# A gated recurrence with a spectral mixing layer on one core: two more chunks in split float32r, gate sums on TensorE, constant matmuls, and another order

## Chip, core and metric

The kernel runs on one core of a Trainium2 chip. The metric is device time in microseconds of one execution; "before" is the median of three runs.

## What is computed

Four batches, eight heads, 768 positions, head size 48 (so 384 channels), all float32. A gated linear attention gives x, and x goes through a mixing layer:

```python
f = 1.0 / (1.0 + np.exp(-f_logit))
for t in range(S):
    state = f[:, :, t, :, None] * state + np.einsum('bhd,bhe->bhde', k[:, :, t], v[:, :, t])
    y[:, :, t] = np.einsum('bhd,bhde->bhe', q[:, :, t], state)
...
theta = x @ w_theta
zr, zi = x * np.cos(theta), x * np.sin(theta)
u = x + einsum('ts,bsd->btd', w_tok_r, zr) + einsum('ts,bsd->btd', w_tok_i, zi)
return u + np.maximum(u @ w_ch, 0.0)
```

The four weight matrices come as 8-byte floats and are turned into 4-byte floats by integer work on the chip.

## The kernel before

The 768 positions of each batch are six chunks of 128, so there are 24 chunks, numbered 0 to 23. Steps have two-letter names. For each chunk the program loads f, k, q and v ("lf", "lk", "lq", "lv"); clamps f from below ("gc", `gate_clamp`); takes log(1 + exp(-f)) ("go", `gate_open`, two ScalarE passes); sums it along the chunk by a VectorE scan ("gs", `gate_sum`); takes the falling and the rising exponential of the sum ("ge", `gate_exp`: `p` and, in place, `f`); multiplies q by the falling one ("gq") and k by the rising one ("gk"). "gp" keeps the last column of the falling product in `pes`. Then TensorE makes scores, key transposes and state sums ("sc", "ke", "up"), VectorE masks the scores and carries the state ("ma", "sa", "st", "sm"), TensorE makes the outputs ("qs", "ou") and turns x ("xt"), and x is kept as it is and turned ("xc", "xs").

The mixing layer's first product is "th" (`angles`), followed by rounding to a turn ("tn", "se", "ab"), sine and cosine ("tr") and the rotation ("ro"), which gives z. The products of z with the two token matrices ("f0", "f1", "f2" for three blocks of 128 channels; `products`) add up in PSUM for a group of 384 positions. VectorE adds them to `ut` ("v", line 462), the sum is split ("uh", "ul"), multiplied by the channel matrix ("c"), and finished and stored ("cv", "so").

A product is made in one of two ways. In plain float32 it is two TensorE instructions. In split form each operand has a high part in float32r and the remainder as a low part, and the product is three float32r matmuls: high by high, high by low, low by high. In the kernel before, `FULL = 1` keeps the whole first batch (chunks 0 to 5) in plain float32, and chunks 6 to 23 in split form. The split needs "xh", "xl" for x, "zh", "zl" for z, and "d4", "d5" for the weights. "d1", "d2", "d3" decode a weight part: shift the low words (VectorE), scale the high words (ScalarE), join (two VectorE instructions).

The order of all this is written out by hand: `ORDER` is a list of steps, and every engine's own queue, the loads on SP's queue among them, follows that list. A suffix /P, /D or /A puts a step on GpSimd (POOL), VectorE (DVE) or ScalarE (ACT). Tiles come from pools with few buffers: PSUM has four single banks (tag "b", used by "ke", "xt", "th", the product groups and "c"), `p` has one buffer, `f`, `k`, `q` and `v` three.

Of the kernel before, what the change touches and what calls it, by code (L numbers as in the profile page):

```python
# [92 lines left out]
def gla_moe_kernel(  # L93
# [111 lines left out]

    def split_hi(n):
        if parts[n][1] and not FULL:
            nc.scalar.mul(place(n, 1), values[n], parts[n][1])
        else:
            copy(nc.scalar, place(n, 1), values[n])  # L210

    def split_lo(n):
        if parts[n][1] and not FULL:
            nc.vector.scalar_tensor_tensor(place(n, 0), values[n], parts[n][1], place(n, 1),
                                           op0=ALU.mult, op1=ALU.subtract)
        else:
            on(nc.vector).tensor_tensor(place(n, 0), values[n], place(n, 1), op=ALU.subtract)
# [481 lines left out]
```

## Time and profile before

| | |
|---|---|
| median of three runs | 340.17 us (339.72 to 340.64) |
| the profiled execution, its own time | 340.03 us |
| its span, first to last instruction | 338.3 us |
| PE (matmul) busy | 320.4 us, 95% |
| DVE busy | 251.6 us, 74% |
| ACT busy | 188.7 us, 56% |
| POOL busy | 108.6 us, 32% |

The span is what the trace shows; the profiled execution's own time is 1.7 us more. A busy share is an average over the whole span. Matmuls overlap, and the trace models their ends, so that PE can read as busy while it waits up to a quarter of a microsecond; the distance from one start to the next tells its pace.

### The profile page before, as it was taken

The page shows a single profiled execution, that of the slowest core. Times are in us where ns is not written, and L with a number is a line of the kernel's source. Part 1 is how long each engine was busy: PE and PEld are TensorE (multiplying, and loading weights), DVE is VectorE, ACT ScalarE, POOL GpSimd, SP SyncE. Part 2 cuts the span into 40 slices and gives each one's busy share as a digit, 9 for nine tenths or more (in the row PEclk, how much of TensorE's full clock was granted, in tenths as well). Part 3 has the DMA queues.
Part 4 walks back from the last instruction along what each step waited for, and adds up shares of the span by engine and source line. Part 5 has one row for each costly group of instructions (what it writes and reads, how often), then busy time and mean ns, then how long its engine had stood idle before and what let it go on. Part 6 is the DMA issues. An engine that isn't in the chain of part 4 may idle for free. (4 is left out here: it accounts for less than half of the span.)

```text
span 338.3 us, 9998 instructions
## 1 busy us (share of the span) xinstructions
PE 320.4 (95%) x4320; PEld 283.2 (84%) x4320; DVE 251.6 (74%) x411; ACT 188.7 (56%) x308; POOL 108.6 (32%) x105
## 2 busy tenths in 40 slices
PE   0789999999999999999999999999999999999993
PEld 0676766776776789999999999999999999999992
DVE  5989999999999998898987857855437848534211
ACT  6787997995866755588476685244076114400010
POOL 3585152134418235701445423323212201300010
PEclk9999999999999999999999999999999999999998
DMA  7994994738761262374124320532121120000012
GB/s 256 382 401 168 317 372 151 249 114 323 244 224 30 64 230 82 91 233 141 33 85 149 122 79 2 187 114 84 40 73 48 47 73 27 0 2 0 11 60 78
DMA packets 21618, 45.54 MB, mean 135 GB/s; under 512 B 2368, under 2 KB 5440, under 8 KB 21568
## 3 DMA queue, kind: packets, MB, share of 16 engines
q1 hardware_dynamic: 21568, 44.84, 38.5%
q8 instruction: 36, 0.59, 0.7%
q14 instruction: 14, 0.11, 0.1%
HBM read 40.11 MB, written 4.72 MB: 133 GB/s over the span
## 5 line engine op out<-in xcount | busy, mean ns | idle before, releaser
L458 PE MATMUL pm<-wp,z 128*128 128x384 f32 x648 | 118.4, 337 | 0.0
L458 PEld LDWEIGHTS pm<-wp,z 128*128 128x128 f32 x648 | 112.4, 188 | 0.4
L458 PE MATMUL pm<-value,z 128*128 128x384 f32 x144 | 49.3, 487 | 0.0
L476 PE MATMUL pch<-uhl,wch 128*128 128x384 f32 x216 | 40.0, 337 | 0.0
L458 PEld LDWEIGHTS pm<-value,z 128*128 128x128 f32 x144 | 26.4, 190 | 15.2
L476 PEld LDWEIGHTS pch<-uhl,wch 128*128 128x128 f32 x216 | 37.4, 188 | 0.0
L469 POOL TENSOR_TENSOR uhl<-ut,uhl 128x384 fp32r<-128x384 f32 x13 | 14.2, 1094 | 67.0 <-ACT uhl L143 35.5
L236 POOL TENSOR_SCALAR f<-f 128x512 f32<-128x512 f32 x16 | 26.6, 1666 | 13.3 <-DMA f<-in_f_dram 12.5
L246 DVE TENSOR_TENSOR_SCAN f<-carry,f 128x512 f32<-128x512 f32 x24 | 29.8, 1246 | 1.4 <-ACT f L242 1.4
L257 POOL COPY pes<-p 128x4 f32<-128x4 f32 x24 | 10.5, 439 | 52.9 <-ACT p L253 52.9
L490 DVE SCALAR_TENSOR_TENSOR ut<-pch,ut 128x384 f32<-128x384 f32 x24 | 13.1, 550 | 18.8 <-PE pch L476 17.1
L308 PE MATMUL psk<-ident,k 128*128 128x128 f32 x96 | 16.9, 303 | 10.0 <-DVE k L266 10.0
L261 POOL TENSOR_TENSOR q<-q,p 128x512 f32<-128x512 f32 x12 | 17.3, 1446 | 23.1 <-ACT p L253 14.6
L462 DVE TENSOR_TENSOR ut<-pm,ut 128x384 f32<-128x384 f32 x24 | 13.0, 551 | 14.2 <-PE pm L458 14.2
L253 ACT ACTIVATE p<-f 128x512 f32<-128x512 f32 x24 | 15.1, 630 | 14.4 <-DVE f L246 6.8
L402 PE MATMUL pth<-wth,xh 128*128 128x384 f32 x108 | 23.0, 348 | 0.0
L308 PEld LDWEIGHTS psk<-ident,k 128*128 128x128 f32 x96 | 12.2, 153 | 12.3 <-issue 10.3
L435 DVE TENSOR_TENSOR w<-w,x 128x768 f32<-128x768 f32 x18 | 17.2, 962 | 6.3 <-ACT w L426 6.3
L143 ACT COPY x<-py 128x384 f32<-128x384 f32 x19 | 9.1, 478 | 22.5 <-PE py L361 22.1
L361 PEld LDWEIGHTS py<-v,sc 64*64 64x64 f32 x768 | 15.0, 140 | 7.4 <-issue 4.5
L143 ACT CAST uhl<-ut 128x384 fp32r<-128x384 f32 x7 | 3.6, 513 | 31.1 <-DVE ut L462 17.5
L266 DVE SCALAR_TENSOR_TENSOR k<-f,k 128x512 f32<-128x512 f32 x24 | 18.2, 758 | 1.8 <-ACT f L254 1.1
(83 smaller groups left out, 622.6 us busy)
## 6 DMA issues: line engine op xcount, KB each, us to landing
v<-in_v_dram SPq DMA_DIRECT2D x24, 384.0 KB, 4.3
f<-in_f_dram SPq DMA_DIRECT2D x24, 256.0 KB, 3.8
q<-in_q_dram SPq DMA_DIRECT2D x24, 256.0 KB, 4.1
k<-in_k_dram SPq DMA_DIRECT2D x24, 256.0 KB, 4.3
raw<-in_w_r_dram SPq DMA_DIRECT2D x12, 384.0 KB, 5.9
raw<-in_w_i_dram SPq DMA_DIRECT2D x12, 384.0 KB, 6.3
out_dram<-ut SPq DMA_DIRECT2D x21, 192.0 KB, 1.9
raw<-in_w_theta_dram SPq DMA_DIRECT2D x3, 384.0 KB, 6.4
```

The source lines that it names most:

```text
L236: on(nc.vector).tensor_scalar(ft, ft, F_MIN, None, op0=ALU.max)
L246: nc.vector.tensor_tensor_scan(fl, carry[:, pairs(h)].rearrange("p n t -> p (n t)"), fl, 0.0, ALU.mult, ALU.add)
L253: nc.scalar.activation(ps_[m][:, pairs(h)], ft, AF.Exp, scale=-1.0)
L261: on(nc.vector).tensor_tensor(qt, qt, ps_[m][:, pairs(h)], op=ALU.mult)
L266: nc.vector.scalar_tensor_tensor(kt, loaded["f", m][:, pairs(h)], E_TOP, kt, op0=ALU.min, op1=ALU.mult)
L308: nc.tensor.transpose(psks[m][:, p, :], loaded["k", m][:, p, :], ident)
L361: nc.tensor.matmul(out[HALF[t], j, p, :], scs[m][HALF[a], j, p, :], v2[HALF[a], t, p, :], start=(t == 0 and m % NC == 0 and p == 0), stop= ...
L402: nc.tensor.matmul(pths[m], l, r, start=(n == 0), stop=(n == len(ms) - 1))
L435: nc.vector.tensor_tensor(zs[m] if full else w, w, xs[m].unsqueeze(1).to_broadcast([P, 2, DM]), op=ALU.mult)
L458: nc.tensor.matmul(pms[g, d], l, r, start=(s == 0 and i == 0), stop=(s == NC - 1 and i == len(ms) - 1))
L469: on(nc.vector).tensor_tensor(us[g, d][:, 0], uts[g][:, d, :], us[g, d][:, 1], op=ALU.subtract)
L476: nc.tensor.matmul(pcs[g, d], l, r, start=(es[0] == 0 and n == 0), stop=(es[-1] == KD - 1 and n == len(ms) - 1))
```

## The change

- `FULL` now counts chunks and is 4: chunks 0 to 3 stay in plain float32, chunks 4 and 5 go the split way. Their weights for "th" and for the token products are split as well.
- `SUMMED = 4`: for chunks 0 to 3 f is loaded in a layout with the position on the partitions (a new input `ft`), and the sum along the chunk is a matmul with a triangle of ones (`upto`), four per chunk. The other chunks keep the scan.
- The clamp is gone. `gate_open` also writes row sums of exp(-f) to `opened`, and the check at the end looks at these too.
- The signs of the two exponentials change places: `p` now holds the rising product for k, `f` the falling one for q and for `pes`.
- `CUT = 1`: the gate work of chunk 0 is done in two halves of two head pairs each ("hlf", "hgo", "hgs" and so on).
- A new step "wu" (`keep_warm`) multiplies two constant tiles into a bank that nobody reads; it stands 30 times in the order.
- v is loaded as three parts of 192 columns, not twice 384: 288 KB a chunk, not 384.
- "d2" and "ro" may go to POOL.
- `ORDER` is new throughout.

```diff
-FULL = 1
-CUT = 0
+FULL = 4
+CUT = 1
+SUMMED = 4
...
     def gate_sum(m, h=None):
+        if m < SUMMED:
+            if not h:
+                sums[m] = bank([P, NP, C], f"psum{m}")
+            for p in range(NP)[pairs(h)]:
+                nc.tensor.matmul(sums[m][:, p, :], loaded["f", m][:, p, :], upto, start=True, stop=True)
+            return
         fl = loaded["f", m][:, pairs(h)].rearrange("p n t -> p (n t)")
...
-    def gate_clamp(m, h=None):
-        ft = loaded["f", m][:, pairs(h)]
-        on(nc.vector).tensor_scalar(ft, ft, F_MIN, None, op0=ALU.max)
...
-        nc.scalar.activation(ft, ft, AF.Exp, scale=-1.0)
+        n = B * NC if h else m
+        nc.scalar.activation(ft, ft, AF.Exp, scale=-1.0, accum_out=opened[:, n:n + 1])
         nc.scalar.activation(ft, ft, AF.Ln, bias=1.0)
...
-        nc.scalar.activation(ps_[m][:, pairs(h)], ft, AF.Exp, scale=-1.0)
-        nc.scalar.activation(ft, ft, AF.Exp)
+        nc.scalar.activation(ps_[m][:, pairs(h)], src, AF.Exp)
+        nc.scalar.activation(ft, src, AF.Exp, scale=-1.0)
...
+    def keep_warm(n):
+        nc.tensor.matmul(bank([P, C], f"warm{n}"), ident, carry[:, 1], start=True, stop=True)
...
-        vs[m] = sb.tile([P, 2, DM], F32, tag="v", bufs=3, name=f"v{m}")
+        vs[m] = sb.tile([P, 3, NP * D], F32, tag="v", bufs=3, name=f"v{m}")
...
-            products(g, s, d, zs[b * NC + s], b < FULL)
+            products(g, s, d, zs[b * NC + s], b * NC + s < FULL)
```

Of the new order three places are shown. The first is the head of PE's queue: `psk` is the transposed keys, `sk` the scores and state sums, `warm` a constant matmul, `psum` a gate sum. Before:

```order
L308 MATMUL psk_131<-ident,k_109 128x128 x4
L322 MATMUL sk<-v_111,ktok_136 64x48 x16
L297 MATMUL sk_156<-q_107,k_109 64x64 x16
L308 MATMUL psk_184<-ident,k_128 128x128 x4
L353 MATMUL py_216<-mid_191,q_107 64x48 x8
```

and now, from the tenth instruction on:

```order
L513 MATMUL warm_136<-carry,ident 128x128
L513 MATMUL warm_138<-carry,ident 128x128
L259 MATMUL psum_141<-upto,f_105 128x128 x4
L513 MATMUL warm_154<-carry,ident 128x128
L259 MATMUL psum_165<-upto,f_108 128x128 x4
L513 MATMUL warm_172<-carry,ident 128x128
L513 MATMUL warm_174<-carry,ident 128x128
L322 MATMUL psk_178<-ident,k_110 128x128 x4
L513 MATMUL warm_186<-carry,ident 128x128
L513 MATMUL warm_188<-carry,ident 128x128
L259 MATMUL psum_193<-upto,f_159 128x128 x4
L513 MATMUL warm_208<-carry,ident 128x128
```

The first key transposes, which opened the queue, now stand behind eleven constant matmuls in a row, two gate sums and three more constant ones.

The second place is the head of DVE's queue, behind its four small fills: `f` is the gate tile, `raw` the loaded words of a weight part (the first is of w_theta), `value` the decoded part. Before:

```order
L236 TENSOR_SCALAR f_92<-f_92 128x512
L236 TENSOR_SCALAR f_95<-f_95 128x512
L246 SCALAR_TENSOR_TENSOR f_92<-carry,f_92 128x512
L246 SCALAR_TENSOR_TENSOR f_95<-carry,f_95 128x512
L261 TENSOR_TENSOR q_107<-q_107,p_114 128x512
L266 SCALAR_TENSOR_TENSOR k_109<-f_92,k_109 128x512
L246 SCALAR_TENSOR_TENSOR f_104<-carry,f_104 128x512
L182 TENSOR_SCALAR raw_125<-raw_125 128x768
L266 SCALAR_TENSOR_TENSOR k_128<-f_95,k_128 128x512
```

and now:

```order
L191 TENSOR_SCALAR raw_96<-raw_96 128x768
L204 SCALAR_TENSOR_TENSOR raw_96<-raw_96 128x768
L205 SCALAR_TENSOR_TENSOR value_99<-raw_96 128x768
L191 TENSOR_SCALAR raw_117<-raw_117 128x384
L283 SCALAR_TENSOR_TENSOR k_110<-p_151,k_110 128x256
L283 SCALAR_TENSOR_TENSOR k_110<-p_151,k_110 128x256
L204 SCALAR_TENSOR_TENSOR raw_117<-raw_117 128x384
L205 SCALAR_TENSOR_TENSOR value_144<-raw_117 128x384
L278 TENSOR_TENSOR q_183<-q_183,f_105 128x256
L152 COPY ktok_199<-psk_178 128x512
L283 SCALAR_TENSOR_TENSOR k_161<-p_205,k_161 128x512
```

Clamps and scans are gone from the head, and the decoding of w_theta, whose load now stands first in SP's queue, has moved ahead of the first key product.

The third place is DVE's queue up to the first addition of a product group to `ut` (`pm` is such a group, `wth`, `wp` and `z` hold split parts). Before:

```order
L193 SCALAR_TENSOR_TENSOR value_986<-raw_901 128x768
L246 SCALAR_TENSOR_TENSOR f_990<-carry,f_990 128x512
L182 TENSOR_SCALAR raw_1165<-raw_1165 128x768
L143 CAST xh_1170<-ut_1122 128x384
L330 TENSOR_TENSOR mid_1176<-sk_1061,st_992 128x192
L334 TENSOR_TENSOR st_1182<-sk_1061,mid_1176 128x192
L246 SCALAR_TENSOR_TENSOR f_1007<-carry,f_1007 128x512
L182 TENSOR_SCALAR raw_1204<-raw_1204 128x768
L462 TENSOR_TENSOR ut_365<-pm_973,ut_365 128x384
```

and now:

```order
L456 TENSOR_TENSOR z_1239<-w_1059,z_1239 128x768
L204 SCALAR_TENSOR_TENSOR raw_1131<-raw_1131 128x768
L205 SCALAR_TENSOR_TENSOR value_1200<-raw_1131 128x768
L456 TENSOR_TENSOR z_1276<-w_1148,z_1276 128x768
L278 TENSOR_TENSOR q_956<-q_956,f_936 128x512
L278 TENSOR_TENSOR q_1084<-q_1084,f_1068 128x512
L343 TENSOR_TENSOR mid_1293<-sk_1112,st_1057 128x192
L347 TENSOR_TENSOR st_1295<-sk_1112,mid_1293 128x192
L191 TENSOR_SCALAR raw_1234<-raw_1234 128x768
L476 TENSOR_TENSOR ut_423<-pm_757,ut_423 128x384
```

The low parts of z for chunks 4 and 5 (line 456) now stand ahead of that addition, and two scans less do.

## Rows read from the trace of the kernel before

**Rows 1.** Busy time by stretch: us, then busy us of each engine, PEclk, DMA share, GB/s.
```profile
0.00:10.00 10.00, 0.45 (x2) 0.48 (x3) 5.90 (x11) 6.82 (x11) 3.06 (x12) 1.00 0.81 278
10.00:20.00 10.00, 8.92 (x207) 7.58 (x210) 9.23 (x16) 7.77 (x14) 7.55 (x7) 1.00 1.02 384
...
30.00:40.00 10.00, 10.00 (x217) 6.62 (x215) 9.38 (x15) 7.98 (x14) 4.67 (x4) 1.00 0.66 201
...
70.00:80.00 10.00, 10.00 (x161) 7.07 (x160) 9.90 (x14) 8.52 (x14) 1.89 (x2) 1.00 0.60 202
...
180.00:200.00 20.00, 20.00 (x336) 19.39 (x335) 14.88 (x23) 15.51 (x26) 9.30 (x8) 1.00 0.35 113
...
330.00:338.30 8.30, 2.64 (x16) 2.31 (x14) 1.64 (x3) 0.00 (x0) 0.19 (x1) 0.80 0.23 79
...
0.00:83.74 83.74, 71.66 (x1149) 49.66 (x1149) 76.17 (x119) 67.39 (x108) 34.07 (x41) 1.00 0.77 275
83.74:338.30 254.56, 248.75 (x3172) 233.54 (x3171) 175.48 (x294) 121.29 (x200) 74.50 (x65) 0.99 0.27 88
```

**Rows 2.** Timeline of PE: start us, us, instruction, count, idle time before it.
```profile
9.55 1.08 PE L308 MATMUL psk<-ident,k 128*128 128x128 f32 x4 [9.55 <-DVE k L266]
...
27.09 4.19 PE L402 MATMUL pth<-value,ut 128*128 128x384 f32 x6
...
34.54 2.20 PE L402 MATMUL pth<-value,ut 128*128 128x384 f32 x6
```

**Rows 3.** Costliest groups of the whole run: count, busy us, mean ns, idle before.
```profile
L458 PE MATMUL pm<-wp,z 128*128 128x384 f32 x648 | 118.4, 337 | 0.0
L458 PE MATMUL pm<-value,z 128*128 128x384 f32 x144 | 49.3, 487 | 0.0
L236 POOL TENSOR_SCALAR f<-f 128x512 f32<-128x512 f32 x16 | 26.6, 1666 | 13.3 <-DMA f<-in_f_dram 12.5
```

**Rows 4.** Groups of DVE from 0 to 83.74 us, the first L462 included.
```profile
L246 DVE TENSOR_TENSOR_SCAN f<-carry,f 128x512 f32<-128x512 f32 x12 | 15.2, 1279 | 1.0 <-ACT f L242 1.0
L193 DVE SCALAR_TENSOR_TENSOR value<-raw 128x768 int32<-128x768 int32 x9 | 8.9, 991 | 0.3
L192 DVE SCALAR_TENSOR_TENSOR raw<-raw 128x768 int32<-128x768 int32 x9 | 8.5, 948 | 0.0
...
L182 DVE TENSOR_SCALAR raw<-raw 128x768 int32<-128x768 int32 x11 | 6.9, 648 | 0.0
L435 DVE TENSOR_TENSOR z<-w,x 128x768 f32<-128x768 f32 x6 | 6.0, 1006 | 0.0
...
L236 DVE TENSOR_SCALAR f<-f 128x512 f32<-128x512 f32 x4 | 1.9, 463 | 2.3 <-DMA f<-in_f_dram 2.3
L409 DVE TENSOR_SCALAR w<-pth 128x384 f32<-128x384 f32 x3 | 1.6, 546 | 0.0
L143 DVE COPY ut<-pxt 128x384 f32<-128x384 f32 x3 | 1.6, 545 | 0.0
...
L143 DVE COPY ktok<-psk 128x512 f32<-128x512 f32 x1 | 0.7, 673 | 0.0
```

**Rows 5.** Groups of DVE of the whole run, for the split of z and of weights.
```profile
L442 DVE TENSOR_TENSOR z<-w,z 128x768 fp32r<-128x768 f32 x13 | 14.3, 1106 | 1.0 <-ACT z L143 0.9
...
L143 DVE CAST wp<-value 128x768 fp32r<-128x768 f32 x3 | 2.3, 776 | 0.0
```

**Rows 6.** Timeline of DVE: its first step on loaded data.
```profile
3.73 0.43 DVE L236 TENSOR_SCALAR f<-f 128x512 f32<-128x512 f32 x1 [2.14 <-DMA f<-in_f_dram]
```

**Rows 7.** DMA issues of the page: count, KB each, median us to landing.
```profile
raw<-in_w_theta_dram SPq DMA_DIRECT2D x3, 384.0 KB, 6.4
```

**Rows 8.** Waits of DVE from 3.7 to 83.7 us: total us, times, longest.
```profile
DVE f L246 <- ACT f L242: 1.0, 2, 0.7
DVE mid L330 <- PE sk L322: 1.0, 1, 1.0
...
DVE mid L328 <- PE sk L322: 0.6, 1, 0.6
DVE sc L303 <- PE sk L322: 0.5, 1, 0.5
```

More of the change, by code (lines that the diff above doesn't have):

```diff
@@ L98, in gla_moe_kernel @@
     f: bass.AP,
+    ft: bass.AP,
     v: bass.AP,
@@ L171, in hold @@
     def hold(n):
-        if FULL and n < NCH:
+        if n < NTOK or n < NCH and (n - NTOK) % NC < FULL:
             tag, bufs = ("uhl", 4) if n < NTOK else ("wp", 25)
@@ L186, in decode_high @@
         low, high = words(n)
-        nc.scalar.activation(high.bitcast(F32), high.bitcast(F32), AF.Copy, scale=2.0 ** -112)
+        if on(nc.scalar) is nc.scalar:
+            nc.scalar.activation(high.bitcast(F32), high.bitcast(F32), AF.Copy, scale=2.0 ** -112)
+        else:
+            on(nc.scalar).tensor_scalar(high.bitcast(F32), high.bitcast(F32), 2.0 ** -112, None, op0=ALU.mult)
     def decode_join(n):
@@ L204, in place @@
         return parts[n][2][i]
+    LATE = [n for n in range(NTOK, NCH) if (n - NTOK) % NC >= FULL]
+    SPLIT = [*range(NTOK), *LATE, *[n for n in range(NTOK, NCH) if n not in LATE]]
     def split_hi(n):
[L207 to L210, printed above, removed]
+        copy(nc.scalar, place(n, 1), values[n])
     def split_lo(n):
[L213 to L217, printed above, removed]
+        on(nc.vector).tensor_tensor(place(n, 0), values[n], place(n, 1), op=ALU.subtract)
     tables = []
@@ L249, in gate_exp @@
         ft = loaded["f", m][:, pairs(h)]
+        src = sums[m][:, pairs(h)] if m < SUMMED else ft
         gate_tables()
@@ L319, in att_state @@
             for j in range(2):
-                h = 2 * p + j
                 for t in range(1 if last_chunk(m) else 2):
                     nc.tensor.matmul(out[HALF[j], t, p, :], kts[m][HALF[t], p, HALF[j]],
-                                     vs[m][HALF[t], 0, h * D:(h + 1) * D], start=True, stop=True)
+                                     vs[m][HALF[t], j, p * D:(p + 1) * D], start=True, stop=True)
     def att_mid(m):
@@ L356, in att_out @@
     def att_out(m):
-        out, v2 = y_of(m), vs[m][:, 1, :].rearrange("s (t p e) -> s t p e", t=2, p=NP)
+        out = y_of(m)
         for n, (p, t) in enumerate(OUT):
@@ L360, in att_out @@
                 j = a ^ t
-                nc.tensor.matmul(out[HALF[t], j, p, :], scs[m][HALF[a], j, p, :], v2[HALF[a], t, p, :],
+                nc.tensor.matmul(out[HALF[t], j, p, :], scs[m][HALF[a], j, p, :],
+                                 vs[m][HALF[a], 2 * j, p * D:(p + 1) * D],
                                  start=(t == 0 and m % NC == 0 and p == 0), stop=(p == NP - 1))
@@ L434, in rotate @@
                 zs[m], zs[m + 1] = two[:, 0], two[:, 1]
-        nc.vector.tensor_tensor(zs[m] if full else w, w, xs[m].unsqueeze(1).to_broadcast([P, 2, DM]), op=ALU.mult)
+        on(nc.vector).tensor_tensor(zs[m] if full else w, w, xs[m].unsqueeze(1).to_broadcast([P, 2, DM]), op=ALU.mult)
     def split_zh(m):
@@ L494, in store @@
         nc.sync.dma_start(out[b, d * P:(d + 1) * P, th * TH:(th + 1) * TH], uts[g][:, d, :])
+    def keep_warm(n):
+        nc.tensor.matmul(bank([P, C], f"warm{n}"), ident, carry[:, 1], start=True, stop=True)
     flag = const.tile([P, 1], I32, tag="flag", name="flag")
-    worst = const.tile([P, 2], F32, tag="worst", name="worst")
+    worst = const.tile([P, 3], F32, tag="worst", name="worst")
     def find_worst(_):
         nc.vector.tensor_reduce(worst[:, 0:1], pes, axis=AX.XY, op=ALU.min)
-        nc.vector.tensor_scalar(worst[:, 1:2], worst[:, 0:1], E_MIN, None, op0=ALU.is_lt)
+        nc.vector.tensor_reduce(worst[:, 1:2], opened, axis=AX.X, op=ALU.max)
+        nc.vector.tensor_scalar(worst[:, 0:1], worst[:, 0:1], E_MIN, None, op0=ALU.is_lt)
+        nc.vector.scalar_tensor_tensor(worst[:, 2:3], worst[:, 1:2], G_TOP, worst[:, 0:1], op0=ALU.is_gt, op1=ALU.add)
         pf = bank([P, 1], "pf")
-        nc.tensor.matmul(pf[:1, :], ones, worst[:, 1:2], start=True, stop=True)
+        nc.tensor.matmul(pf[:1, :], ones, worst[:, 2:3], start=True, stop=True)
         nc.vector.tensor_copy(flag[:1, :], pf[:1, :])
@@ L514, in go @@
                 loaded[nm, m] = sb.tile([P, NP, C], F32, tag=nm, bufs=bufs, name=f"{nm}{m}")
-            nc.sync.dma_start(loaded[nm, m][:, pairs(h)], src[m // NC, m % NC][:, pairs(h)])
+            rows = ft[m] if nm == "f" and m < SUMMED else src[m // NC, m % NC]
+            nc.sync.dma_start(loaded[nm, m][:, pairs(h)], rows[:, pairs(h)])
         return go
     def load_v(m):
-        vs[m] = sb.tile([P, 2, DM], F32, tag="v", bufs=3, name=f"v{m}")
+        vs[m] = sb.tile([P, 3, NP * D], F32, tag="v", bufs=3, name=f"v{m}")
         nc.sync.dma_start(vs[m], v[m // NC, m % NC])
@@ L524, in inner, with later @@
         return lambda n: fn(n // (NC - 1) * NC + n % (NC - 1))
-    def later(fn, per, first=FULL):
-        return lambda n: fn(n + first * per)
+    def later(fn, first):
+        return lambda n: fn(n + first)
     def piece(d):
@@ L542, in gla_moe_kernel @@
     by_halves = {
-        "lf": load("f", f, 3), "lk": load("k", k, 3), "lq": load("q", q, 3), "gc": gate_clamp, "go": gate_open,
+        "lf": load("f", f, 3), "lk": load("k", k, 3), "lq": load("q", q, 3), "go": gate_open,
         "gs": gate_sum, "ge": gate_exp, "gq": gate_q, "gk": gate_k,
@@ L546, in gla_moe_kernel @@
     fn = {"h" + s: lambda n, go=go: go(n // 2, n % 2) for s, go in by_halves.items()}
-    fn |= {s: later(go, 1, CUT) for s, go in by_halves.items()}
+    fn |= {s: later(go, CUT) for s, go in by_halves.items()}
     fn |= {
         "lv": load_v, "lw": load_part,
-        "d1": decode_low, "d2": decode_high, "d3": decode_join, "d4": split_hi,
-        "di": decode_scale, "d5": split_lo,
+        "d1": decode_low, "d2": decode_high, "d3": decode_join, "d4": lambda n: split_hi(SPLIT[n]),
+        "di": decode_scale, "d5": lambda n: split_lo(SPLIT[n]),
         "e4": lambda n: split_hi(NCH + n), "e5": lambda n: split_lo(NCH + n),
@@ L555, in gla_moe_kernel @@
         "st": inner(att_new), "sm": inner(att_fade), "qs": att_old, "ou": att_out, "xc": att_x, "xt": att_turn, "xs": keep_x,
-        "xh": later(lambda m: split_xh(m, u_slice(m)), NC), "xl": later(lambda m: split_xl(m, u_slice(m)), NC),
-        "th": lambda m: angles(m, m < FULL * NC), "tn": whole, "se": settle, "ab": fold, "tr": trig,
-        "ro": lambda m: rotate(m, m < FULL * NC), "zh": later(split_zh, NC), "zl": later(split_zl, NC),
+        "xh": later(lambda m: split_xh(m, u_slice(m)), FULL), "xl": later(lambda m: split_xl(m, u_slice(m)), FULL),
+        "th": lambda m: angles(m, m < FULL), "tn": whole, "se": settle, "ab": fold, "tr": trig,
+        "ro": lambda m: rotate(m, m < FULL), "zh": later(split_zh, FULL), "zl": later(split_zl, FULL),
         "f0": piece(0), "f1": piece(1), "f2": piece(2), "v": group(add_u), "uh": group(split_uh), "ul": group(split_ul), "c": channels, "cv": group(finish),
-        "so": group(lambda g, d: store(g // NTH, g, d)), "fl": find_worst,
+        "so": group(lambda g, d: store(g // NTH, g, d)), "fl": find_worst, "wu": keep_warm,
     }
@@ L659, in rows @@
         return np.ascontiguousarray(t.transpose(0, 3, 2, 1, 4))
+    f = rows(inputs["f_logit"])
     v = np.asarray(inputs["v"])
@@ L664, in layout @@
     halves = v.transpose(0, 2, 1, 3).reshape(B, NC, 2, HF, NP, 2, D)
-    rolled = np.stack([np.stack([halves[:, :, t, :, :, a ^ t] for t in range(2)], axis=3) for a in range(2)], axis=2)
-    v2 = np.stack([halves.reshape(B, NC, C, DM), rolled.reshape(B, NC, C, DM)], axis=3)
-    v2 = np.ascontiguousarray(v2)
+    parts = [halves[..., 0, :], halves[..., 1, :], halves[:, :, ::-1, :, :, 1, :]]
+    v2 = np.ascontiguousarray(np.stack([a.reshape(B, NC, C, NP * D) for a in parts], axis=3))
     return {
@@ L670, in layout @@
         "k": rows(inputs["k"]),
-        "f": rows(inputs["f_logit"]),
+        "f": f,
+        "ft": np.ascontiguousarray(f.reshape(B * NC, P, NP, C)[:SUMMED].transpose(0, 3, 2, 1)),
         "v": v2,
```

17 lines of the change are left out of this document (11 added, 6 removed), and 72 rows, old and new, of the table ORDER.

## The prediction

> **What bounds the kernel now.** I read the stretches first, then PE's timeline, the groups, and DVE's waits. Read the stretches [rows 1] by column. PE does next to nothing in the first 10 us, is busy without a break from 30 us on, and ends in the last stretch. So from about 31 us to the end every microsecond of PE work is a microsecond of time. DVE is the second full engine: 9.23, 9.38 and 9.90 us of 10 in three of the stretches up to 80 us, but only 14.88 of 20 at 180 us. Two regimes follow. Up to about 84 us DVE and PE are packed together, and work taken off one of them alone need not help; later only PE counts. I cut the run at one place that both kernels have, the first addition of a product group to `ut`. Before it, DVE is busy 76.17 of 83.74 us; behind it 254.56 us are left, of which PE is busy 248.75 [rows 1].
>
> The head hides a third thing. Four key transposes from 9.55 us take 1.08 us, and the six angle matmuls at 27.09 us take 4.19 us, while the same six at 34.54 us take 2.20 [rows 2]. [...] The clock rose right behind a full-width stretch, the angle matmuls.
>
> **Products on PE.** A matmul of 384 columns occupies PE for 49.3/144 = 0.342 us in plain float32 and 118.4/648 = 0.183 us in float32r [rows 3]. One "f" step (a chunk, a block of channels) is four of the first kind, 1.37 us, or six of the second, 1.10 us. Two chunks, two groups and three blocks make 12 steps, so the split saves 12 x 0.27 = 3.2 us in all. A gate sum or a constant matmul moves 128 columns in two instructions: a third of 0.342 each, 0.23 us a matmul at the higher clock, 0.46 at the lower. The 16 gate sums add 3.7 us and the 30 constant ones 6.9 us. All the sums and 24 of the constants stand ahead of the place, most in the head, where PE is idle or waits: I cost them at nothing. If that cover is gone they cost up to 9.2 us (40 x 0.23).
>
> **DVE up to the place.** I count the instructions ahead of the addition in both orders and price them from [rows 4] and [rows 5]. Gone: six scans of twelve, 6 x 1.279 = 7.7; four clamps, 1.9; two roundings from `pth`, 1.1; one copy to `ut`, 0.5; one rotation, 1.0. Sum 12.2. Come in: one more join of a weight part, counted as three first halves more and one second half less, 3 x 0.948 - 0.991 = 1.9; a cast of a token part, 0.8, and one half its size, 0.4; one copy to `ktok`, 0.7; two low parts of z, 2 x 1.106 = 2.2. Sum 6.0. A few short ones of both signs (a fold less, half a q product more, a longer low part for a shorter one) cancel. Net: **-6.2 us**, or -5.7 when I allow 0.5 us for what the halved k products cost twice.
>
> **DVE's start.** Its first step on data was the clamp at 3.73 us [rows 6]. Now it is the shift of w_theta's words, behind two loads of 384 KB in place of one of 256. The extra 512 KB take 1.3 us at 384 GB/s, the rate from 10 to 20 us [rows 1]. Low end: 0.5 us, if the second load lands right behind the first. High end: w_theta took 6.4 us from issue to landing under load [rows 7], which from an issue at about 1.3 us is 4 us later than before. I take **+1.2**, near the low end, since only gate loads share the queue at that time.
>
> **DVE's waits up to the place.** The scans' wait for ACT, 1.0 us, goes with them. The waits for PE's `sk`, 1.0, 0.6 and 0.5 [rows 8], fall in the head, where PE ran at half its pace; with the higher clock I let them go, -2.1. New is a wait of the first join for POOL, which now scales the high words: no row shows that on POOL. Its clamp of 512 columns takes 1.666 us [rows 3], so 768 would be 2.5 us, against 0.65 us of shifting on DVE meanwhile [rows 4]: +1.9. Low end zero, high end 4, if the second part's scaling holds up a join as well. Together -1.0 - 2.1 + 1.9 = **-1.2**; between -3 and +3.
>
> **PE behind the place.** The new order leaves three "f" steps more behind it: two plain ones (2.74 us) and one split (1.10), +3.8. Seven split steps that already stood behind it save 7 x 0.27 = 1.9. Two constant matmuls in the middle add 0.5; the last four run behind the last channel products, beside DVE's last adds and the store, and cost nothing. Sum **+2.4**.
>
> **Other edits.** ACT is busy 67.39 of 83.74 us up to the place [rows 1]; row sums of the exponential and the extra high parts have 16 us of idle time to lie in. POOL is at 34.07 of 83.74, and its eight clamps there (8 x 1.666 = 13 us) make room for three scalings, two low parts and a rotation. The smaller loads of v and the larger check at the end touch no full engine. Without POOL's cover, a late state fade would come back as a DVE wait, which the range holds.
>
> **Sum.** -5.7 + 1.2 - 1.2 + 2.4 = -3.3. The profiled execution took 340.03 us (span 338.3, and 1.7 around it; its median of runs is 0.14 higher), so I predict **336.7 us**.
>
> **Rivals.** *First: DVE is no longer the bound.* DVE's 5.7 us, its 2.1 us of waits on a slow PE and all 3.2 us of products count, less 1.2 for the start and 0.5 for constants: -9.3, 330.7. For it: at 27 us PE spends 4.19 us on what takes 2.20, and gate sums let it start early. Against it: DVE at 9.90 of 10 us around 75 us [rows 1] cannot be run past. Half of it, 331 to 335, is likelier than all.
>
> *Second: nothing is left.* The new order puts more DVE work ahead of the twelfth chunk's key product than the old: four shifts, three joins, four token casts and two low parts of z more (2.6 + 5.8 + 3.1 + 2.2), four scans and four clamps fewer (-5.1 - 1.9), and some eight short ones of 0.4 to 1 us, about +10 us in all by [rows 4] and [rows 5]. PE has about as much less left behind it: five "f" steps (5 to 6 us), an angle product and one chunk's scores and state sums have moved ahead. If PE waits there, DVE's +10 and PE's -10 cancel and the later start of 1.2 us remains: 341.2, or 340 with the waits gone. For it: both engines are full up to the place [rows 1], so DVE's count decides. Against: not every DVE step ahead of those keys has to come before them.
>
> [...]
>
> [...]
>
> **How the numbers follow.** A measurement of this kernel tells 0.3%, about 1.0 us, from no change. Forecast (336 to 339): 0.45. First rival (331 to 336): 0.24. Second (339 to 341.2): 0.19. Third (above 341.2): 0.12. Faster by over 0.3% are the first two, less a little: 0.68; within 0.3% the second and the forecast's edge: 0.19; slower 0.13. The range 332.0 to 341.2 leaves out the third rival and the far end of the first.
>
> **What would show it.** Right: DVE's first addition to `ut` near 80 us (83.74 - 5.7 + 1.2 - 1.2 = 78), PE busy about 257 us behind it, angle matmuls of chunk 0 in 2.2 us instead of 4.19, and split products with `z` of chunks 4 and 5 at 0.18 us each. Wrong: PE waiting for DVE (`k`, `z`) between 80 and 130 us, as in the second rival; gate sums at 0.23 us an instruction, as in the third; a join that waits for POOL by more than 2 us; or the low words of w_theta landing after 6 us.

## The result, and the profile after

The changed kernel takes **343.38 us** (median of 4 runs, 342.0 to 344.7) against 339.95 of the kernel before on the same chip: ratio 1.0111, interval 1.0073 to 1.0148. It is slower by 3.4 us where 3.3 us less was forecast. Its profiled execution took 344.36 us, span 342.2. Ratios, here and below, compare the fast runs alone, each set with its own runs of the kernel before, so a ratio need not be the quotient of two medians.

The stretches, columns as in [rows 1]; the first three rows end at the first addition to `ut`, the place of the prediction:

```profile
0.00:30.00 30.00, 24.77 (x471) 21.25 (x472) 20.92 (x38) 21.76 (x46) 18.19 (x26) 1.00 0.86 308
30.00:70.00 40.00, 35.58 (x639) 24.95 (x640) 33.80 (x54) 33.28 (x58) 12.59 (x13) 0.96 0.72 232
70.00:84.82 14.82, 14.82 (x214) 11.72 (x210) 14.68 (x23) 11.92 (x20) 3.10 (x3) 1.00 0.65 217
...
0.00:84.82 84.82, 75.18 (x1307) 57.92 (x1311) 69.40 (x113) 66.96 (x122) 33.88 (x41) 0.98 0.76 256
84.82:342.20 257.38, 251.01 (x3147) 238.84 (x3139) 170.90 (x282) 120.70 (x207) 92.91 (x79) 0.99 0.26 83
```

The same cuts in the kernel before:

```profile
0.00:30.00 30.00, 18.01 (x328) 14.32 (x329) 24.12 (x39) 23.13 (x38) 15.43 (x23) 1.00 0.90 334
30.00:70.00 40.00, 39.92 (x653) 26.38 (x652) 38.45 (x62) 33.67 (x54) 13.75 (x14) 1.00 0.69 238
```

DVE is busy 69.40 us up to the place, 6.8 less than before [rows 1]: the work did go. But DVE is idle for 15.42 us there (84.82 - 69.40) against 7.57, and the place comes 1.1 us later, not 5.7 earlier. Of the 7.85 us of new idle time, 3.2 lie in the first 30 us (9.08 against 5.88) and 4.65 between 30 and 70 us (6.20 against 1.55). PE too, without a pause from 30 to 70 us before, now stands for 4.4 us there. The waits of DVE up to the place (total, times, longest), which answer to [rows 8]:

```profile
DVE raw L191 <- DMA raw<-in_w_theta_dram: 3.2, 1, 3.2
DVE k L283 <- ACT p L270: 2.7, 2, 2.0
DVE raw L204 <- POOL raw L199: 2.1, 1, 2.1
DVE mid L343 <- PE sk L335: 1.3, 1, 1.3
DVE sc L317 <- PE sk L335: 1.2, 1, 1.2
```

The timeline of PE tells why PE stands:

```profile
36.21 0.40 PE L335 MATMUL sk<-v,ktok 64*64 64x48 f32 x12
37.95 0.55 PE L335 MATMUL sk<-v,ktok 64*64 64x48 f32 x20 [1.34 <-issue]
38.43 2.20 PE L416 MATMUL pth<-value,ut 128*128 128x384 f32 x6
...
43.49 0.69 PE L311 MATMUL sk<-q,k 48*64 48x64 f32 x30
46.66 0.27 PE L311 MATMUL sk<-q,k 48*64 48x64 f32 x2 [2.48 <-issue]
...
47.88 3.46 PE L416 MATMUL pth<-value,ut 128*128 128x384 f32 x6
```

Read the two bracketed rows. Each stop lies inside a run of 32 equal products whose operands are all there: 30 of the scores' products run, nothing happens for 2.48 us, then the last two. "issue" is time in which the engine waited for nothing that the profile shows. Behind the second stop the granted clock falls to 0.50 (from 49 to 51 us; 0.92 from 40 to 50 as a whole, 0.91 from 50 to 60), and the angle matmuls need 3.46 us for what takes 2.20 at 38.43. The two DVE waits for `sk` end behind the two stops (38.55 and 47.50 us). The long wait for `p` comes later by a chain: PE's late outputs hold up ACT's copy `x`, ACT's queue stands behind it, and DVE's k product behind that. ACT:

```profile
53.68 0.48 ACT L152 COPY x<-py 128x384 f32<-128x384 f32 x1 [4.20 <-PE py L374]
54.17 1.28 ACT L234 ACT_TABLE_LOAD   x1
55.47 0.63 ACT L270 ACTIVATE p<-f 128x512 f32<-128x512 f32 x1
```

and DVE:

```profile
56.13 0.69 DVE L283 SCALAR_TENSOR_TENSOR k<-p,k 128x512 f32<-128x512 f32 x1 [2.03 <-ACT p L270]
```

The kernel before had a stop of the same kind, in a row that the prediction passed over:

```profile
21.70 1.10 PE L322 MATMUL sk<-v,ktok 64*64 64x48 f32 x31 [1.05 <-issue]
```

Part of the rest came about as announced. In this execution the head is quick on PE, with a granted clock of 1.00 on record from 7.5 us: chunk 0's angle matmuls take 2.20 us, against 4.19 [rows 2].

```profile
22.34 2.20 PE L416 MATMUL pth<-value,ut 128*128 128x384 f32 x6
```

The split products stand in their groups, at 0.187 us each where 0.183 was priced, and the plain ones at 0.356 against 0.342:

```profile
L472 PE MATMUL pm<-wp,z 128*128 128x384 f32 x720 | 134.7, 339 | 0.0
L472 PE MATMUL pm<-value,z 128*128 128x384 f32 x96 | 34.2, 493 | 0.0
```

So the two groups together are busy 168.9 us, against 167.7 [rows 3]: these rows do not show the 3.2 us saved. A group's busy time also holds the modelled ends of its matmuls. Counted instead from each product's start to the start of the next matmul, over all of the trace, the products take 158.45 us against 160.88, so 2.4 us were saved. The kernel now ends with PE's constants instead of DVE's last add (the chain that ended last):

```profile
335.88 0.47 PE warm L513 x2
```

### The profile page after: what moved, and what is told of

It is laid out like the page before. It is cut to its first block, busy times and chain, and to the rows that moved or that the text cites. A ratio compares the mean times of both kernels' runs of the same rounds, so it can differ in the third digit from the quotient of the medians.

```text
span 342.2 us, 10309 instructions
## 1 busy us (share of the span) xinstructions
PE 326.2 (95%) x4442; PEld 296.8 (87%) x4442; DVE 240.3 (70%) x393; ACT 187.7 (55%) x329; POOL 126.8 (37%) x119
## 5 line engine op out<-in xcount | busy, mean ns | idle before, releaser
L472 PE MATMUL pm<-wp,z 128*128 128x384 f32 x720 | 134.7, 339 | 0.0
L476 DVE TENSOR_TENSOR ut<-pm,ut 128x384 f32<-128x384 f32 x24 | 13.2, 552 | 31.1 <-PE pm L472 31.1
L472 PE MATMUL pm<-value,z 128*128 128x384 f32 x96 | 34.2, 493 | 0.0
L407 POOL TENSOR_TENSOR xl<-ut,xh 128x384 fp32r<-128x384 f32 x14 | 18.7, 1334 | 37.4 <-DVE xh L152 21.3
L456 POOL TENSOR_TENSOR z<-w,z 128x768 fp32r<-128x768 f32 x10 | 20.6, 2058 | 15.1 <-DVE z L152 13.6
L283 DVE SCALAR_TENSOR_TENSOR k<-p,k 128x512 f32<-128x512 f32 (+1 forms) x25 | 18.8, 754 | 8.2 <-ACT p L270 4.5
L416 PEld LDWEIGHTS pth<-wth,xh 128*128 128x128 f32 x120 | 21.0, 188 | 0.9 <-ACT ktok L152 0.2
L278 POOL TENSOR_TENSOR q<-q,f 128x512 f32<-128x512 f32 (+1 forms) x14 | 20.2, 1442 | 3.3 <-ACT f L271 2.5
L311 PE MATMUL sk<-q,k 48*64 48x64 f32 x768 | 16.9, 221 | 3.5 <-issue 2.5
L374 PEld LDWEIGHTS py<-v,sc 64*64 64x64 f32 x768 | 14.2, 133 | 6.2 <-issue 3.4
L249 ACT ACTIVATE f<-f 128x512 f32<-128x512 f32 (+1 forms) x25 | 15.3, 611 | 5.8 <-DMA f<-in_ft_dram 3.7
L311 PEld LDWEIGHTS sk<-q,k 48*64 48x64 f32 x768 | 14.1, 135 | 5.0 <-issue 4.2
```

Source lines behind the costliest of these rows:

```text
L249: nc.scalar.activation(ft, ft, AF.Exp, scale=-1.0, accum_out=opened[:, n:n + 1])
L278: on(nc.vector).tensor_tensor(qt, qt, loaded["f", m][:, pairs(h)], op=ALU.mult)
L283: nc.vector.scalar_tensor_tensor(kt, ps_[m][:, pairs(h)], E_TOP, kt, op0=ALU.min, op1=ALU.mult)
L311: nc.tensor.matmul(out[HALF[j ^ t], j, p, :], kt[r, p, HALF[t]], qt[r, p, HALF[t]], start=True, stop=True)
L374: nc.tensor.matmul(out[HALF[t], j, p, :], scs[m][HALF[a], j, p, :], vs[m][HALF[a], 2 * j, p * D:(p + 1) * D], start=(t == 0 and m % NC == ...
L407: on(nc.vector).tensor_tensor(xls[m], src, xhs[m], op=ALU.subtract)
```

## The experiments

Theory B: PE stops at fixed counts of its own instructions, and the order now puts such a stop into runs of small products. Theory A: the head starves DVE. Rivals: a collision with loads, and the constants' own PE time or clock. Steps are named as in the order (`wu` a constant matmul, `lw` a load of weights, `d1`, `d2`, `d3` the shift, scaling and join of their words, `lf`, `lk` loads, `go`, `gs`, `ge` the gate steps, `/P` on POOL, `h` half a chunk). All kernels but one are the changed one with the edit shown; the kernel before had a median of 339.5 to 340.1 us in each set.

**What the constants cost.** Three kernels take some of them out.

```diff
e2_tail
-c rv cv wu wu cv cv so wu wu
+c rv cv cv cv so
e4_nowarm
-wu   (all 30)
e8_eleven
-wu   (all but the first 11)
```

> The changed kernel without the last four constant matmuls. Theory 'fetch': they keep PE from its end by 1.4 us, so that its last instruction transfer comes behind the 576 KB store; without them the time from the last finishing add to the end falls from 6.9 us to the 5.6 us of before, 1.0 to 1.4 us faster. Theory 'idle': they run beside DVE's last adds and the store and cost nothing, within 0.3 us.

Measured 341.8 us (ratio 1.006, 1.003 to 1.009), 1.6 less than the changed kernel. The two intervals overlap, but the traces agree with the medians. DVE's last additions, in the changed kernel, in e2_tail and in the kernel before:

```profile
334.15 1.67 DVE L504 SCALAR_TENSOR_TENSOR ut<-pch,ut 128x384 f32<-128x384 f32 x3 [3.08 <-PE pch L490]
335.42 1.67 DVE L504 SCALAR_TENSOR_TENSOR ut<-pch,ut 128x384 f32<-128x384 f32 x3 [3.08 <-PE pch L490]
331.63 1.67 DVE L490 SCALAR_TENSOR_TENSOR ut<-pch,ut 128x384 f32<-128x384 f32 x3 [3.08 <-PE pch L476]
```

From their end to the end of the span it is 6.4 us (342.2 - 335.8) with the four constants, 4.8 without them (341.9 - 337.1), and 5.0 before. The last four constants were costed at nothing and cost that.

> The changed kernel without any constant matmul. [...] Theory 'DVE': the head waits for DVE anyway, and the whole is up to 1.5 us faster, by the tail and by the constants' own time. Rival 'gate sums warm enough': the clock rises with the gate sums, and the head differs by under 1 us.

Measured 339.45 us (0.9998, 0.9967 to 1.0028): 3.9 less than the changed kernel, where no theory gave more than 1.5. No wait on "issue" is left on PE, and DVE is busy 39.65 us of the 40 between 30 and 70.

> The changed kernel with only the first 11 of its 30 constants, those that run before 10 us. Theory B (constants cost where PE is full or where they move PE's instruction count; in an idle head they only lift the clock): 338.5 to 339.8, the angles of chunk 0 in 2.2 us, no wait of PE of 2 us amid the scores products near 44 us, since that run of products now ends before PE's 1473rd instruction. Rival (the 11 cost their share, by a chip that falls back in clock behind them or by later first steps): 340.5 to 342, with granted clock under 0.95 in a stretch before 60 us.

Measured 338.85 us (0.9946, 0.9917 to 0.9976): faster than the kernel before, 4.5 us less than the changed kernel. Behind the head one stop is left, and in PE's timeline it lies elsewhere, amid an angle product:

```profile
46.41 0.66 PE L322 MATMUL psk<-ident,k 128*128 128x128 f32 x4
46.91 0.81 PE L416 MATMUL pth<-value,ut 128*128 128x384 f32 x2
48.48 1.45 PE L416 MATMUL pth<-value,ut 128*128 128x384 f32 x4 [0.76 <-issue]
```

So far the constants could be at fault themselves. The next kernels part the loads, the constants and the count.

**Loads or count.** e1_spread moves four of the eight loads of 384 KB that meet with the stop to later steps (and a shift and a scaling with them):

```diff
-ge lw kt qs ou lw lw lw ro/P ... tr lv kt d1 d2 xc gs xt ge ro
+ge lw kt qs ou lw ro/P ... tr lv lw kt d2 xc gs xt ge lw ro
```

> The changed kernel with two of its token-weight loads (and one shift and one scaling of the first of them) put later in the order, so that four loads no longer follow each other. Theory 'fetch': PE's idle 2.48 us at 44 us, in the middle of a run of equal matmuls that wait for nothing, is PE waiting for its own instructions, whose transfer stands behind those loads; it then goes (under 0.5 us), the lower clock from 48 to 52 us goes with it, the sixth mask (58.6 us) comes 3 to 5 us earlier, and the whole is 1.5 to 4 us faster. Theory 'DVE' (DVE's count of work bounds up to 130 us): the idle time may go, DVE waits less, but the whole moves by under 1 us. [...]

Measured 344.09 us (1.0111, 1.0071 to 1.0151), and a stop of 2.11 us at the same two products. But this does not clear the loads. In the trace the eight are still issued close together, from 39.1 to 44.8 us (36.8 to 42.2 in the changed kernel), and at the stop, which begins at 44.91 us, DMA is as full as ever (share 1.03):

```profile
44.00:46.00 2.00, 0.91 (x33) 0.60 (x32) 1.97 (x4) 1.98 (x3) 0.28 (x1) 1.00 1.03 376
```

e14_shift48 is e8_eleven with twelve one-column matmuls (`wt`) ahead of the first transposes and behind the third gate sum; e17_small is e2_tail with the middle fifteen constants made one column wide:

```diff
+    def shift(n):
+        nc.tensor.matmul(bank([P, 1], f"shift{n}")[:64], ident[:64, :64], carry[:64, 1, :1], start=True, stop=True)
e14_shift48
-gs d3 di d4 ke ... di gs hlq kt/D
+gs d3 di d4 wt wt wt wt wt wt ke ... di gs wt wt wt wt wt wt hlq kt/D
e17_small
-wu
+wt   (the twelfth to the twenty-sixth)
```

> The kernel with the first 11 constants (338.85 when measured), and twelve matmuls of one column and 64 rows ahead of the first transposes and behind the third gate sum, where PE waits anyway: 48 instructions of some 0.03 us each, 1 us of PE in all. They put PE's instructions at the same count as in the changed kernel, so that the stop that this kernel has ahead of an angle product (0.76 us near 48) falls into the run of 64 small products of scores and state sums. [...] Rival (the later constants cost PE time or clock, the count is nothing): no such stop, 338.5 to 339.5.

Measured 344.83 us (1.0133, 1.0097 to 1.0168): 6 us for twelve matmuls of nearly no work. In PE's timeline the stop is where it was foretold, at the border of scores and state sums of chunk 4:

```profile
47.75 0.69 PE L311 MATMUL sk<-q,k 48*64 48x64 f32 x32
50.56 0.67 PE L335 MATMUL sk<-v,ktok 64*64 64x48 f32 x16 [2.11 <-issue]
```

Not all of the 6 us is the stop's: 2.1 us are lost before chunk 3's mask, where the head ran at a lower clock for longer (granted clock 0.70 from 10 to 20 us and 0.79 from 20 to 30, against 0.66 and 1.00 in e8_eleven), and 3.4 between the masks of chunks 3 and 5.

> The changed kernel without its last four constants (341.8 when measured), the middle fifteen replaced in place by matmuls of one column and 64 rows: the same number of PE instructions, 0.2 us less PE time for each. Theory B (the count): the stop of 2 to 3 us amid the scores of chunk 4 stays, 341 to 342. Rival (the middle constants' PE time, fifteen of 0.23, or the clock behind them): 338.5 to 339.5.

Measured 345.44 us (1.0143, 1.0099 to 1.0186), with stops of 0.87, 0.79 and 3.03 us. The time is 3.4 us above theory B's range, and why is open. But with less PE time in the constants the kernel is slower, not faster: their time is not what they cost. Last, the opposite, e18_middle: the fifteen stay in full, and the count is moved by leaving out the first eleven (and the last four).

> The changed kernel without its last four and without its first eleven constants: only the fifteen in the middle stay. 44 PE instructions fewer ahead of chunk 4's scores, so that PE's stop falls behind the run of small products, at the angle product, as in the kernel with the first eleven alone. Theory B (the count): the masks of chunks 3 and 5 stand 15 to 16.5 us apart instead of 18.7 to 21.5, no stop of 2 us, and 339 to 340.5 us, although the fifteen are all there. Rival (the fifteen constants themselves cost 3 us): 341.5 to 343, the two masks 18 us apart or more.

Measured 338.55 us (0.9951, 0.9927 to 0.9976), a little under theory B's range. The fifteen are all there and the loss is gone; the masks came 16.9 us apart, a little over the range, since PE waited 2.4 us for ACT. So the fifteen do not cost 3 us by themselves. The work between two stops shows the count. PE's matmuls and weight loads from one stop to the next, in the changed kernel:

```profile
37.90:44.20 6.30, 6.23 (x127) 4.16 (x128) 5.46 (x10) 4.70 (x10) 4.25 (x5) 1.00 0.96 310
```

in e17_small (two such stretches):

```profile
31.85:38.10 6.25, 5.18 (x127) 3.81 (x126) 5.36 (x9) 5.59 (x10) 0.54 (x2) 1.00 0.92 309
38.85:45.15 6.30, 6.23 (x127) 4.16 (x128) 5.57 (x10) 5.08 (x11) 4.69 (x5) 1.00 0.96 327
```

and in e14_shift48:

```profile
42.20:50.50 8.30, 6.23 (x127) 4.16 (x127) 8.13 (x14) 6.86 (x13) 4.96 (x5) 1.00 0.90 314
```

253 to 255 records each time, whatever the stretch holds. Counted from the program's start the place is the same too: in the changed kernel and nine of the others (e1, e2, e8, e10 to e13, e17, e19) the longest stop behind the head comes behind 726 matmuls and 727 weight loads, whatever their heads and constants, and in e14_shift48 behind 3 records more. The changed kernel and e8_eleven up to that stop:

```profile
0.00:46.60 46.60, 37.15 (x726) 29.84 (x727) 35.66 (x61) 36.65 (x72) 25.59 (x32) 1.00 0.89 307
0.00:48.40 48.40, 38.01 (x726) 29.91 (x727) 37.84 (x62) 36.68 (x72) 26.45 (x32) 0.93 0.84 290
```

The traces also hold the transfers of instructions. Here are those of the whole changed kernel, 37 packets (0.61 MB, 16 KB each), and the one that starts between 44.2 and 44.3 us, just behind the beginning of the long stop at 44.18:

```profile
q8 instruction: 37, 0.61, 0.7%
q8 instruction: 1, 0.02, 60.1%
```

That packet takes 0.96 us (60.1% of 16 engines' 0.1 us), and PE goes on 1.4 us after its end. So do the others: each of the 19 stops behind the first 10 us, in 13 traces, ends 1.30 to 1.55 us after the end of such a packet. The loads may well make the packet late. This one starts 6.3 us after PE went on from the stop before, with DMA nearly full (share 0.96, above). Later, between 110 and 221 us, nine packets find DMA at a share of 0.25 or less. If the places of the stops are counted on in steps of 254, an estimate from the records above, seven of them start 0.6 to 1.1 us after such a place, and two up to 26 records ahead of one. No run takes the loads away, so their part stays open.

What a stop costs shows in the time from the mask of chunk 3 (L317) to that of chunk 5. In the first five rows the granted clock fell behind the stop (mean of 40 to 60 us 0.83 to 0.92), in the others it did not (1.00):

| kernel | longest stop, us, where | masks 3 to 5, us | median, us |
|---|---|---|---|
| changed kernel | 2.5, scores | 19.4 | 343.38 |
| e1_spread | 2.1, scores | 18.7 | 344.09 |
| e2_tail | 3.3, scores | 21.5 | 341.8 |
| e14_shift48 | 2.1, state sums | 18.9 | 344.83 |
| e17_small | 3.0, scores | 21.0 | 345.44 |
| e8_eleven | 0.8, angles | 15.5 | 338.85 |
| e13_gates_shift (below) | 1.0, angles | 15.7 | 338.09 |
| e18_middle | 0.2, angles | 16.9 | 338.55 |
| e4_nowarm | none | 15.0 | 339.45 |

**The head.** e4_nowarm has no stop and is still not faster than before: DVE stands for 10.25 us of the first 20, against 4.87 in [rows 1].

```diff
e6_head (no constants)
-lw d1 hlf hlf lf hlk hgo lw d2/P d3 hgo hlk hgs d1 d2/P hgs go hge hge
+hlf hlf lf hlk hgo hlk lw hgo lw hgs hgs go hge hge d1 hgk hgk d2 ... d3
e7_scan (no constants)
-SUMMED = 4
+SUMMED = 0
e9_noclamp (the kernel before)
-gc gc/P   (all)
```

> The changed kernel without its 30 constant matmuls, and with another head: the two half loads of the gates and the first two loads of k go ahead of w_theta's, the first two high words are scaled on ACT instead of POOL, and the first two joins stand behind the first k products. Theory A (the gain was lost in the first 20 us: DVE stands idle for 10.25 us there against 4.87 in the kernel before, and is full from 30 to 80 us): the gates are opened some 1.7 us earlier, the first k product stands near 8.5 us instead of 10.67, the first addition to ut comes 2 to 3 us earlier than at 83.9, and the time falls from 339.45 to 336.5 to 337.5. Rival (what counts is only how much DVE has to do, and DVE is behind by then anyway): the idle time moves to another wait in the first 30 us, and the time stays at 339 to 340.

Measured 342.73 us (1.0076, 1.0045 to 1.0107), worse than either theory said. With five loads ahead of w_theta DVE has nothing to do at all; the first of its waits (total, times, longest):

```profile
DVE raw L190 <- DMA raw<-in_w_theta_dram: 7.7, 1, 7.7
```

> The changed kernel without its 30 constants and with all gate sums taken by the scan on DVE, as in the kernel before (four more scans, 5 us of DVE by 1.28 each, and no triangular matmuls). Theory A (DVE's work up to the place and its waits in the head set the time): the four scans come back on DVE in full or nearly so, 342.5 to 344.5. Rival (the sums on PE, 2 us of PE at the lower clock for each four and a wait of ACT behind them, hold up the head as much as they save on DVE): 339 to 340.5.

Measured 346.77 us (1.0195, 1.0161 to 1.023), 7.3 more than with the sums on PE, and beyond theory A's range. It is more than the scans' own time, since the first keys come later and PE stands: `psk` waits 14.2 us for DVE, and the granted clock is 0.66 from 30 to 40 us. The gate sums on PE are worth having. (e5_scan, the same with the constants left in, gave no time.)

> The kernel before without its twelve clamps of the gates at -44 (left out; the state of the gates is otherwise the same). Four of them stand on DVE, 0.43 each, eight on POOL. Theory A (DVE is the bound up to the first addition to ut): 1.7 us less on DVE and an earlier first step: 337.5 to 338.5. Rival (DVE's time in the head is hidden behind the loads): 339.2 to 340.

Measured 339.43 us (1.0002, 0.9972 to 1.0032): the rival. The four clamps on DVE (1.9 us of the prediction's sum) lay in time in which DVE waited anyway; the scan behind them then waited 3.8 us for ACT.

Four kernels then feed DVE earlier, on top of e8_eleven:

```diff
-lw d1 wu wu hlf hlf lf hlk wu hgo lw d2/P d3 hgo
e10_act
+lw d1 wu wu hlf hlf lf hlk wu d2 hgo lw d3 hgo
e11_gates
+hlf hlf lw d1 wu wu lf hlk wu hgo hgo lw d2 d3
e12_act_shift, e13_gates_shift (as e10 and e11, and)
-gk lv up sa st ... gq/P lw ke sc kt d1
+gk lv lw d1 up sa st ... gq/P ke sc kt
```

> The changed kernel with its first 11 constants only (338.85 when measured alone) and the first high word of w_theta scaled on ACT, ahead of the first gate step, instead of on POOL. Theory A (DVE's idle time in the first 20 us, 10.2 us against 4.87 in the kernel before, is what is left of the loss, and the join's wait for POOL, 2.1 us, is part of it): the first join begins near 6.7 instead of 8.25 us, the first k product 1 us earlier, the first addition to ut near 81.8, and the time 337.3 to 338.3. Rival (the gate steps, 0.9 us later on ACT, hold up the first k product instead): 338.7 to 340.

Measured 341.78 us (1.0026, 0.9994 to 1.0059), its runs, one of 801 us aside, spread from 338.5 to 344.3. Its timeline of ACT:

```profile
4.94 1.28 ACT L197 ACT_TABLE_LOAD   x1 [4.94 <-DMA raw<-in_w_theta_dram]
6.24 0.90 ACT L197 ACTIVATE raw<-raw 128x768 f32<-128x768 f32 x1
7.16 1.28 ACT L234 ACT_TABLE_LOAD   x1
8.45 0.42 ACT L249 ACTIVATE f<-f 128x256 f32<-128x256 f32 x1
```

The scaling ahead of the gates loads a table of its own, and the gates load theirs behind it. The first gate step stands at 8.45 instead of 5.83 us, and DVE's k products wait 3.4 us for `p`. The rival had such a delay, of 0.9 us, but not the tables, and the median lies above both ranges.

> As the kernel with the first 11 constants only, but the two half loads of the gates go ahead of w_theta's first two, and both first high words are scaled on ACT behind the two half gate steps. Theory A: the gates are opened near 4.3 us instead of 5.83, w_theta lands 0.7 us later, the first join begins near 7.5, the first k product near 9.6 instead of 10.6: 336.8 to 338.3. Rival (DVE's first step waits for w_theta, and every 0.1 us that it lands later is lost): 339 to 340.

Measured 338.2 us (0.9958, 0.9929 to 0.9988): theory A's range, by 0.65 us less than e8_eleven in the median, which the intervals don't tell apart. The scaling behind the half gate steps needs no table of its own: ACT loads one, 1.28 us at 0.80, ahead of both, and none between the gate steps and the scaling at 6.48.

> As e10_act, with the third load of weights and its shift on DVE (0.55 us) moved ahead of the first state sums' steps, where DVE waited 1.6 us for PE's state sums. Theory A: 0.4 to 0.6 us less than e10_act. Rival (the wait is for PE, which waits for DVE's k: the shift only delays it): the same as e10_act or slower.

Measured 339.98 us (1.0029, 0.9995 to 1.0064): not told apart from e10_act.

> As e11_gates, with the third load of weights and its shift moved ahead of the first state sums' steps as in e12_act_shift. Theory A: 0.4 to 0.6 us less than e11_gates. Rival: the same as e11_gates or slower.

Measured **338.09 us** (0.994, 0.9897 to 0.9983), not told apart from e11_gates. Its stretch up to the place, which stands at 79.3 us:

```profile
0.00:79.30 79.30, 70.20 (x1277) 53.80 (x1281) 70.26 (x112) 67.42 (x123) 31.52 (x40) 1.00 0.80 274
```

DVE is idle for 9.0 us there. This profiled execution took 336.72 us, among the fastest of the kernel's seven (336.3 to 342.8); the median is not told apart from e8_eleven's. Three more tried to improve on it:

```diff
e15_none (e13_gates_shift)
-wu   (all)
e16_eight (e13_gates_shift)
-wu wu wu wu wu wu wu wu hlk hgs
+wu wu wu wu wu hlk hgs
e19_middle_gates
+the head of e13_gates_shift in e18_middle
```

> e13_gates_shift without any constant. Theory A (with DVE fed early the head is bound by DVE, and the clock in it gives little): 338 to 339, no stop of PE for its own instructions. Rival (the lifted clock in the first 10 us is what lets the k products and scores start early): 340 to 341, first scores 2 us later.

> e13_gates_shift (338.1) with eight constants instead of eleven: 12 PE instructions fewer, so that the stop of 0.98 us near 44 us, amid an angle product, falls behind that product, whose 2 us then cover it. Theory B: the stop shrinks below 0.4 us and the time is 337 to 338. Rival (the stop goes wherever it is put, or the three constants are missed in the head): 338 or more.

> e18_middle (338.55: the fifteen middle constants, neither the first eleven nor the last four) with the head of e13_gates_shift (the half loads of the gates ahead of w_theta, the first high words scaled on ACT behind the half gate steps, the third weight shift ahead of the first state sums). Theory A (DVE's idle time in the head is the other part of the loss): DVE's first addition to ut near 80 us, 336 to 337.5. Rival (without the first eleven constants the head is slow on PE, as in e15_none): 338.5 to 340.

Measured, in this order: 339.98 us (1.001, 0.9986 to 1.0035), 340.5 (1.0015, 0.9994 to 1.0036) and 339.26 (0.9998, 0.997 to 1.0027). The first lies at the edge of its rival's range, the other two in theirs. In e16_eight the stop is gone from PE's waits, as theory B said, and the time is still 2.4 us more. That would fit a head that needs all of the first eleven constants, but this is not shown: e19_middle_gates has none of them, and in its profiled execution (337.36 us) the place comes at 79.45 us, as early as in e13_gates_shift. e13_gates_shift keeps the lowest median, some 1.8 us below the kernel before, and is not told apart from e8_eleven, e11_gates and e18_middle.

## Why the prediction was wrong

- **DVE's work, -5.7: right.** Measured -6.8. But e9_noclamp shows that the clamps in that sum were worth nothing in time. Of its signs, the first addition near 78 us did not come (84.8), and the join's wait for POOL over 2 us did (2.1).
- **DVE's start, +1.2: right.** 4.78 us against 3.73, +1.05.
- **DVE's waits, -1.2: the step that failed.** Busy time fell by 6.8 and idle time rose by 7.85; less the start, that is +6.8. The join's wait for POOL is the 1.9 foreseen (2.1). The waits for `sk` were let go because of the clock, rightly for the head, but two new ones of 1.3 and 1.2 us stand behind PE's stops, and the wait for `p` behind them is 2.0. In all 4.65 of the 7.85 us lie from 30 to 70 us, where no DVE wait was expected, and the kernels without the long stop pass that stretch some 4 us faster (table). Some 2 us more are short waits for loads and ACT in the head.
- **"All the sums and 24 of the constants stand ahead of the place ... I cost them at nothing": wrong, but not by the cover.** The price was looked for in PE time (up to 9.2 us). e18_middle and e17_small show that the time of the middle fifteen is not what cost; their number is.
- **PE behind the place, +2.4: near.** 257.38 against 254.56, +2.8. The products gave back 2.4 of 3.2 us in all, by their starts. "The last four cost nothing" failed: 1.6 us by e2_tail, so the other terms came out some 1.2 us lower than forecast. The constants themselves end at 336.4 us, and what they hold up behind that no row shows.
- **The rivals.** The third was put above 341.2 us, and that is where the time lies, but its sign, gate sums at 0.23 us an instruction, did not come (eight in 1.16 us at 8.93). In the profiled execution PE stopped first, and the granted clock fell, to 0.50, behind the stop. In other executions with the same eleven constants ahead the clock was lower in the head (granted clock from 10 to 20 us 0.83 in e1_spread, 0.66 in e8_eleven), and e8_eleven is faster than the kernel before all the same. The second rival, a twelfth chunk whose keys hold up PE, did not happen: PE is busy all of 70 to 84.82 us, and has no wait from 80 to 130.
- **The clock up to 31 us.** The prediction took the times of PE's matmuls (4.19 us, then 2.20) for a lower clock that rose, against a granted clock of 1.00 in [rows 1]. That 1.00 is no measurement: the trace of the kernel before has no record of the clock ahead of 31.1 us, and a stretch without one reads 1.00. So no run shows the clock of that stretch, on which the 0.46 us of a matmul and the -2.1 for waits on `sk` rest; both were the author's estimate. What the runs show is the pace: chunk 0's six angle matmuls in 2.20 us here, with 1.00 on record, against 4.19 before, and chunk 4's six in 3.46 us, most of them where 0.50 is on record (48.5 to 51.9 us).

The changed kernel's trace has 8884 matmul and weight-load records, some 35 steps of 254, and two such stops, so most steps pass without one. The stops cost 0.2 us (e18_middle) to 1.0 us (e13_gates_shift) amid angle products, and up to 3.3 us (e2_tail) amid small ones. That PE waits there for its own instructions is read from the count, which follows the edits, and from the packet that ends 1.30 to 1.55 us ahead of each stop's end; no row names PE's wait for it.

With the stop shortened and DVE fed earlier, e13_gates_shift comes near the forecast's picture: the place at 79.3 us (78 forecast). That its profiled execution took just the forecast 336.7 us is luck, since the median is 338.1. How much of the remaining gap is the head's is not shown.

## What to carry to other kernels

In a trace, look for "<-issue" inside a run of equal instructions: here it was no dependency but recurred by count, and adding or removing a few dozen instructions ahead moved it (48 in e14_shift48), so an edit's time can change by some 4 us for reasons that have nothing to do with the edit. Put long matmuls, not a run of small ones, where the count falls (stops of 0.2 to 1.0 us against up to 3.3 here), and vary the count before judging a new order. An edit that is to spread loads has to be looked up in the trace: in e1_spread they stood as close as before. And work taken off a full engine is worth time only where that engine does not wait: here the clamps gave nothing, while five loads ahead of w_theta's cost 3.3 us (e6_head against e4_nowarm).

## What was not expected of the hardware

- PE stopped, in these traces, at steps of 253 to 255 of its matmul and weight-load records, longest amid small products: 1.05 us in the kernel before, up to 3.3 us here. Each stop ends 1.30 to 1.55 us after a 16 KB packet of instructions.
- A stop of 2.48 us amid dense work was followed by a granted clock of 0.50 from 49 to 51 us, as above. Twelve matmuls of one column, ahead of the place that they shift, cost 6 us, 3.4 of them between the two masks.
- Taking a row sum along on ACT is an instruction of its own, 0.19 us, behind each exponential of a gate step, here in ACT's timeline of e8_eleven:

```profile
5.83 0.42 ACT L249 ACTIVATE f<-f 128x256 f32<-128x256 f32 x1 [3.75 <-DMA f<-in_ft_dram]
6.16 0.19 ACT L249 ACTIVATION_READ_ACCUMULATOR f<-f 128x1 f32 x1
```
